# One table of a scan-and-MLP kernel: the clamp, the second block's first steps, two masks and the accumulator banks

## The chip, the cores and the metric

The kernel runs on one core of one Trainium2 chip. The core has a matrix engine (TensorE, PE in the profile, with its weight loads as PEld), three engines for elementwise work (VectorE or DVE, ScalarE or ACT, GpSimd or POOL), and a queue engine, SyncE or SP, that only issues DMAs. ScalarE and GpSimd can issue DMAs too. Each engine works through its own instruction stream in order and waits on semaphores for the others. The metric is the device time of one execution in microseconds (us).

## The reference

The inputs are a state-space scan followed by a squared-ReLU MLP. The scan is taken over chunks of 32 positions in the reference, with the state carried from chunk to chunk:

```python
log_a = np.log(np.clip(a, 1e-06, 1.0))
for c in range(nc):                                  # batch 4, 8 heads, 768 positions, head_dim 32, d_state 16
    cum = np.cumsum(la, axis=-1)
    L = np.exp(cum[:, :, :, None] - cum[:, :, None, :]) * causal
    y_intra = np.einsum('bhij,bhjd->bhid', np.einsum('bhin,bhjn->bhij', Cc, Bc) * L, xc)
    y_inter = np.einsum('bhin,bhnd->bhid', Cc, state) * np.exp(cum)[:, :, :, None]
    y[:, :, sl] = y_intra + y_inter
    state = decay_full[:, :, None, None] * state + np.sum(Bx, axis=2)
# y becomes 3072 tokens x 256; w_in is 256 x 2048, w_out 2048 x 256
h = np.maximum(x @ w_in, 0.0)
return (h * h @ w_out).astype(np.float32)
```

## The kernel before

**Tiling.** The work is cut into 12 units, each a batch and a stretch of 256 positions (`UNITS`). The first four units are the first stretch of the four batches. Each unit goes through a scan stage and then an MLP block; the blocks are lettered a to l, so block a is unit 0 and block b is unit 1.

**The order.** The string `ORDER` is the schedule, written out by hand. It is read token by token, and each token records its instructions on their engines. What stands earlier in the string stands earlier in the stream of each engine it uses, so the string sets the order on every engine and on every DMA queue. Nothing reorders it.

**The scan stage of a unit k**, by tokens:
- `ldC`, `ldB`, `ldx`: loads on SP's queue. `pc`, `pb`, `px`: GpSimd (or the engine named behind a colon: `v` VectorE, `a` ScalarE, `p` GpSimd) scales C by the running product of a, casts B, and divides x by that product, into the tiles jt and xs.
- `tr`, `tc`: PE transposes jt into a PSUM bank, and two engines copy it out to bct (L205, L220, L218).
- `mt`: the scores C·B, 16 matmuls (L235) into banks 0 to 3. Each bank has then to be multiplied by the causal mask. `mk` does it on VectorE straight from PSUM (L244). `sc` followed by `ms` does it in two steps: ScalarE copies the bank out (L249), and the engine named behind `ms` multiplies the copy (L253).
- `u`: 16 matmuls that give the unit's contribution to the state. `ina` and `inb`: 32 matmuls of masked scores with xs. `sf`: VectorE scales the state (tile Sd, L383). `ca`: two matmuls that add the carried state (all L260).
- `t`: two copies that take the result out of PSUM as the tile T, the input of the MLP block. `us`: the copy of the state.

**The MLP block**, by tokens: `b0` is step 0 of block b, four matmuls of 128x256 (L450) into one bank and the ReLU on ScalarE (L459, tile hb); `qb0` is the square on VectorE (L465, tile h); `B0` is the four matmuls with w_out (L481). A block has eight steps. Steps 0 and 1 use the first quarter of w_in (`w_in_b0`), steps 2 and 3 the second (`w_in_b1`), and so on.

**The weights** come in eight DMAs on GpSimd's queue, `wi0` to `wi3` (L148) and `wo0` to `wo3` (L152).

**The later rows of a.** Units 0 to 3 need only the first 64 rows of `a`. The other rows come in four small DMAs and are then prepared once: `ac1` clamps them (L604, GpSimd, tile a_cl), `sk1` takes the running product (L533, VectorE, tile cp), `pp1` picks the last column (L608, ScalarE), `p2` turns them on PE in fp32 (L507, L511, L620), and `pd` copies the result out (L626, L627, ScalarE).

**The banks.** `pp` is all of PSUM, eight banks of 512 fp32. `bank()` gives out the bank that has been free longest, in the order of the string. A digit behind `@` names the bank instead, and `u0:67` names the pair of banks of a `u`. `id` tokens are matmuls of ones, whose result nobody uses, that stand between the first steps.

Of the kernel before, what the change touches and what calls it, by code (L numbers as in the profile page):

```python
# [30 lines left out]
def kernel(  # L31
# [16 lines left out]
    ORDER = """  # L48
        fa1:a jz0:v ef jz1:p id3:512 ti fa0:s la0:s id4:512 pi eb ldB0:s ac0:v ldC0:a sk0 ku sp la1:a pbh0:p hd
        id1:256 pc0:v pbl0:v mb:a id2:512 trC0 ps iv:8:16 tcC0:1:a tcC0:0:v trB0 la2:s tcB0:2:v pk id1:512 iv1:0:8  # L50
        id1:512 ldx0:s mt0 wi0 la3:s px0:v ldC1:s ac1:p su id2:512 ldB1:s wi1 ldx1:s u0:67 mk0 fq mk0 mk0 pc1:p sc0
        pb1:a tr1 id2:512 tc1:1:a tc1:0:v jz2:a to ms0:p sf0 sk1 wo0 wi2 px1:p mt1 ina0 inb0 ca0 mk1 mk1 t0:aa sc1 us0
        pp1:a mk1 a0 ldC2:s a1 u1 ina1 ms1:v wo1 wi3 pc2 inb1 p2 pd sf1 ca1 t1:va us1 a3 qa1 ldB2:s qa0 a2 wo2 b0 qa3
        qb0 b1 qb1 fr b2 b3 A0 A1 B0 pb2:p B1 tr2 zb0 qb3 gB3:v ldx2:s ldB3:s ldC3:s ldx3:s b4 a4 iv:32:64 zb1 tc2:1:v
        qa2 tc2:0:v b5 sb1 sb0 qb4 a5 qb2 qa4 mt2 sc2 B3 iv:16:32 px2 mk2 mk2 sc2 A3 A2 ms2:v qa5 a6 b6 ms2:p B2 a7
        qb5 pb3:a qa6 b7 u2 ina2 inb2 sf2 wo3 pc3 px3 ld4 A4 tr3 ca2 tc3:1:v t2:aa B4 us2 B5 tc3:0:v u3:45 pc4 mt3 A5
        us3 sc3 c5 qb7 qb6 mk3 za3 pb4 ldC5:s ldB5:s c3 qa7 c4 qc5 c0 qc3 px4 tr4 ldx5:s pb5 pc5 sa3 c1 c6 ldC6:s tr5
        ldB6:s ldx6:s qc4 qc0 A6 px5 pq A7 wm c2 B6 c7 C0 ms3:v mk3 qc6 mk3 qc7 afC2 pc6 B7 C3 C6 C4 qc1 bk rg4 C1 qc2
        d1 d0 za4 sa4 pb6 mk4 mk4 d3 mk4 C5 d4 qd0 d2 mk4 px6 tr6 ld7 C2 C7 qd1 qd2 qd3 zb3 rg5 sb3 D0 mk5 za5 sa5 D1
        mk5 d5 qd4 D2 pc7 pb7 d6 qd5 d7 qd6 D3 zb2 e0 qd7 mk5 e1 qe0 sb2 D4 mk5 D5 tr7 ld8 e2 qe1 D6 e3 qe2 ml px7 rg6  # L60
        e4 D7 qe3 za6 sa6 zb6 mk6 e5 qe4 sb6 e6 qe5 e7 qe6 iv:64:96 mk6 E0 E1 E2 E3 ldC9:s ldB9:s px8 mk6 f0 qe7 E4 f1
        qf0 pc8 E5 pb8 tr8 ldx9:s E6 mk6 f2 qf1 f3 qf2 E7 rg7 mk7 F0 f4 qf3 za7 F1 F2 f5 qf4 f6 qf5 f7 qf6 g0 qf7 zb7
        sa7 sb7 mk7 F3 mk7 F4 pc9 pb9 tr9 px9 ld10 g1 qg0 F5 mk7 g2 qg1 zb4 sb4 F6 g3 qg2 F7 rg8 za8 zb8 sa8 sb8 g4
        qg3 G0 mk8 g5 qg4 G1 mk8 g6 qg5 G2 g7 qg6 G3 mk8 h0 qg7 G4 pc10 pb10 tr10 px10 ld11 h1 qh0 G5 mk8 zb5 sb5 h2
        qh1 G6 h3 qh2 G7 rg9 za9 zb9 sa9 sb9 h4 qh3 H0 mk9 h5 qh4 H1 mk9 h6 qh5 H2 h7 qh6 H3 mk9 i0 qh7 H4 pc11 pb11
        tr11 px11 i1 qi0 H5 mk9 i2 qi1 H6 i3 qi2 H7 rg10 za10 zb10 sa10 sb10 i4 qi3 I0 mk10 i5 qi4 I1 mk10 i6 qi5 I2
        i7 qi6 I3 mk10 j0 qi7 I4 j1 qj0 I5 mk10 j2 qj1 I6 j3 qj2 I7 rg11 za11 zb11 sa11 sb11 j4 qj3 J0 mk11 j5 qj4 J1
        mk11 j6 qj5 J2 j7 qj6 J3 mk11 k0 qj7 J4 k1 qk0 J5 mk11 k2 qk1 J6 k3 qk2 J7 rg12 k4 qk3 K0 k5 qk4 K1 k6 qk5 K2
        k7 qk6 K3 l0 qk7 K4 l1 ql0 K5 l2 ql1 K6 l3 ql2 K7 l4 ql3 L0 l5 ql4 L1 l6 ql5 L2 l7 ql6 L3 ql7"""
# [803 lines left out]
```

## Time and profile before

| | us |
|---|---|
| median of 3 runs | 114.66 |
| lowest and highest run | 114.01, 114.71 |
| the profiled execution's own time | 114.46 |
| its span in the profile | 112.8 |
| PE busy in the span | 107.3 |
| VectorE, ScalarE, GpSimd busy | 83.8, 77.0, 51.9 |

The span runs from the first instruction to the last. The profiled execution took 1.66 us more than its span and 0.20 us less than the median run. Busy time on PE is modelled from starts, so a busy PE isn't a PE at its peak. In a merged row of the timeline, several like instructions in a row stand as one, with their count behind an x.

### The profile page before, as it was taken

The page shows a single profiled execution, that of the slowest core. Times are in us where ns is not written, and L with a number is a line of the kernel's source. Part 1 is how long each engine was busy: PE and PEld are TensorE (multiplying, and loading weights), DVE is VectorE, ACT ScalarE, POOL GpSimd, SP SyncE. Part 2 cuts the span into 40 slices and gives each one's busy share as a digit, 9 for nine tenths or more (in the row PEclk, how much of TensorE's full clock was granted, in tenths as well). Part 3 has the DMA queues.
Part 4 walks back from the last instruction along what each step waited for, and adds up shares of the span by engine and source line. Part 5 has one row for each costly group of instructions (what it writes and reads, how often), then busy time and mean ns, then how long its engine had stood idle before and what let it go on. Part 6 is the DMA issues. An engine that isn't in the chain of part 4 may idle for free.

```text
span 112.8 us, 3680 instructions
## 1 busy us (share of the span) xinstructions
PE 107.3 (95%) x1450; PEld 92.3 (82%) x1450; DVE 83.8 (74%) x187; ACT 77.0 (68%) x158; POOL 51.9 (46%) x97
## 2 busy tenths in 40 slices
...
GB/s 39 196 192 180 188 216 202 130 195 182 149 164 58 117 255 97 112 173 74 109 167 76 179 140 83 143 147 110 184 123 0 6 96 0 21 78 0 93 0 93
DMA packets 67281, 13.44 MB, mean 119 GB/s; under 512 B 63104, under 2 KB 65984, under 8 KB 67264
## 3 DMA queue, kind: packets, MB, share of 16 engines
...
q10 hardware_dynamic: 1280, 0.23, 1.1%
q8 instruction: 11, 0.18, 0.8%
q14 instruction: 6, 0.05, 0.1%
...
## 4 chain that ended last, share of the span: by engine, by line
PE 74%; DMA 13%; SPq 6%; issue 3%; POOL 2%; ACT 0%; ACTq 0%; POOLq 0%
PE pp L481 34%; PE pp L450 32%; DMA x_nat<-in_x_dram 13%; PE pp L260 5%; SPq L134 4%; PE pp L229 2%; SPq L642 1%; PE pp L235 1%; POOL xs L187 1%; POOL jt L167 1%; SPq L117 0%; PE pp L205 0%; ACT osl L831 0%; POOL w_out_b L152 0%; POOL mts L253 0%
## 5 line engine op out<-in xcount | busy, mean ns | idle before, releaser
L459 ACT ACTIVATE hb<-pp 128x512 bf16<-128x512 f32 x96 | 54.8, 602 | 22.9 <-PE pp L450 22.6
L465 DVE TENSOR_TENSOR h<-hb 128x512 bf16<-128x512 bf16 x96 | 46.0, 494 | 13.9 <-ACT hb L459 13.3
L450 PE MATMUL pp<-T,w_in_b 128*128 128x256 bf16 x384 | 53.4, 273 | 1.2 <-ACT us L336 0.6
L481 PE MATMUL pp<-w_out_b,h 128*128 128x256 bf16 (+1 forms) x400 | 53.8, 268 | 0.0
L450 PEld LDWEIGHTS <-w_in_b 128*128 128x128 bf16 x384 | 41.4, 114 | 3.2 <-issue 1.3
L481 PEld LDWEIGHTS <-h 128*128 128x128 bf16 x400 | 37.6, 98 | 4.5 <-issue 1.0
L244 DVE TENSOR_TENSOR mts<-pp,mask 128x512 bf16<-128x512 f32 x43 | 28.6, 679 | 0.8 <-PE pp L229 0.8
L187 POOL TENSOR_TENSOR xs<-x_nat,Pinv 128x256 bf16<-128x256 f32 (+1 forms) x19 | 13.6, 727 | 11.4 <-PE pp L260 7.1
L371 POOL TENSOR_TENSOR Sd<-z,Pquad 128x256 bf16<-128x256 f32 x16 | 10.7, 678 | 15.0 <-DVE z L355 8.7
L167 POOL TENSOR_TENSOR jt<-C_nat,P_sb 128x128 bf16<-128x128 f32 x22 | 9.7, 463 | 6.0 <-DMA C_nat<-in_C_dram 6.0
L355 DVE SCALAR_TENSOR_TENSOR z<-z,Ptot,us 128x64 f32<-128x64 f32 x8 | 3.2, 406 | 5.6 <-ACT us L339 4.4
L540 PE MATMUL pp<-const-bfloat16-1.0 128*128 128x512 bf16 (+1 forms) x16 | 6.2, 520 | 0.8 <-PEq L857 0.8
L175 POOL CAST jt<-B_nat 128x256 bf16<-128x256 f32 x9 | 4.5, 505 | 5.0 <-DMA B_nat<-in_B_dram 5.0
L488 ACT COPY osb<-pp 128x512 f32<-128x512 f32 x11 | 6.4, 585 | 0.3 <-PE pp L481 0.2
L260 PE MATMUL pp<-mts,xs 64*32 64x128 bf16 (+1 forms) x288 | 5.5, 219 | 0.0
L260 PE MATMUL pp<-bct,Sd 128*128 128x128 bf16 x40 | 4.2, 220 | 0.0
L260 PEld LDWEIGHTS <-xs 64*32 64x32 bf16 (+1 forms) x288 | 3.6, 93 | 0.4 <-issue 0.2
L540 PEld LDWEIGHTS <-const-bfloat16-1.0 128*128 128x128 bf16 x16 | 1.6, 119 | 2.3 <-issue 2.2
L260 PEld LDWEIGHTS <-Sd 128*128 128x128 bf16 x40 | 3.0, 98 | 0.3
L148 POOL DMA_DIRECT2D w_in_b<-in_moe_w_in_dram x4 | 3.1, 782 | 0.3 <-issue 0.3
L249 ACT CAST sc<-pp 128x512 bf16<-128x512 f32 x5 | 2.9, 610 | 0.2 <-PE pp L235 0.2
L205 PEld LDWEIGHTS <-jt 128*128 128x128 bf16 x24 | 1.7, 104 | 1.6 <-POOL jt L167 0.8
...
## 6 DMA issues: line engine op xcount, KB each, us to landing
...
```

Source lines behind the costliest of these rows:

```text
L134: (eng or nc.sync).dma_start(out=t[what][:, hs[0]:hs[1]], in_=_dap(src, ((b * NH + hs[0]) * S + j * 256) * w, [[2 * w, 128], [S * w, hs[1] ...
L167: eng.tensor_tensor(out=_fap(jt[k % 3], 128 + 144 * g, [[384, 2], [32, 4], [1, 16]]), in0=_fap(loaded[k]["C"], 128 * g, [[16, 2], [32, 4], ...
L187: eng.tensor_tensor(out=_fap(xs, 256 * r, [[256, 2 // n], [32, 8], [1, 32]]), in0=_fap(loaded[k]["x"], 32 * r, [[32, 2 // n], [64, 8], [1, ...
L244: nc.vector.tensor_tensor(out=live[k]["mts"][:, q].rearrange("p r g i -> p (r g i)"), in0=pp[:, q, :], in1=mask1 if k >= LATE else mask, o ...
L260: nc.tensor.matmul(dst, w, v, start=bool(need), stop=False, skip_group_check=True, **({} if pos is None else {"tile_position": pos}))
L371: nc.gpsimd.tensor_tensor(out=_fap(S_d, 0, [[128, 2], [32, 4], [1, 32]]), in0=_fap(z, 0, [[32, 2], [0, 4], [1, 32]]), in1=_fap(Pquad, 4 * ...
L450: nc.tensor.matmul(pp[:, h, i * 256:(i + 1) * 256] if c is None else _fap(pp, h * 512 + i * 256 + c * 64, [[128, 2], [1, 64]]), _fap(w, g ...
L459: nc.scalar.activation(out=hb.rearrange("p i t -> p (i t)"), in_=pp[:, h, :], func=AF.Relu)
L465: nc.vector.tensor_tensor(out=h2, in0=hb, in1=hb, op=ALU.mult)
L481: nc.tensor.matmul(dst, h2[:, i, r * 128:(r + 1) * 128], w_out_b[gi][:, 2 * o + i, c0:c1], start=first, stop=(fp == 7 and i == 1), skip_gr ...
L488: nc.scalar.copy(out=osb, in_=pp[:, 6 if blk == 1 else 7, :])
L540: nc.tensor.matmul(pp[:, h, 0:int(cols)], ones_b[:, 0:128], ones_b[:, 0:int(cols)] if dep is None else dep, start=True, stop=True, skip_gr ...
```

## The change

Only the table `ORDER` is changed. It has 557 tokens before and after. The new table is a line longer, so every later line number goes up by one: L450 of before is L451 of the change.

```diff
-        id1:512 ldx0:s mt0 wi0 la3:s px0:v ldC1:s ac1:p su id2:512 ldB1:s wi1 ldx1:s u0:67 mk0 fq mk0 mk0 pc1:p sc0
-        pb1:a tr1 id2:512 tc1:1:a tc1:0:v jz2:a to ms0:p sf0 sk1 wo0 wi2 px1:p mt1 ina0 inb0 ca0 mk1 mk1 t0:aa sc1 us0
-        pp1:a mk1 a0 ldC2:s a1 u1 ina1 ms1:v wo1 wi3 pc2 inb1 p2 pd sf1 ca1 t1:va us1 a3 qa1 ldB2:s qa0 a2 wo2 b0 qa3
-        qb0 b1 qb1 fr b2 b3 A0 A1 B0 pb2:p B1 tr2 zb0 qb3 gB3:v ldx2:s ldB3:s ldC3:s ldx3:s b4 a4 iv:32:64 zb1 tc2:1:v
-        qa2 tc2:0:v b5 sb1 sb0 qb4 a5 qb2 qa4 mt2 sc2 B3 iv:16:32 px2 mk2 mk2 sc2 A3 A2 ms2:v qa5 a6 b6 ms2:p B2 a7
-        qb5 pb3:a qa6 b7 u2 ina2 inb2 sf2 wo3 pc3 px3 ld4 A4 tr3 ca2 tc3:1:v t2:aa B4 us2 B5 tc3:0:v u3:45 pc4 mt3 A5
+        id1:512 ldx0:s mt0 wi0 la3:s px0:v ldC1:s su id2:512 ldB1:s wi1 ldx1:s u0:67 mk0 fq mk0 mk0 pc1:p sc0 pb1:a
+        tr1 id2:512 tc1:1:a tc1:0:v jz2:a to ms0:p ac1:p sf0 wo0 px1:p wi2 mt1 ina0 inb0 ca0 mk1 mk1 t0:aa sc1 us0 mk1
+        a0 a1@1 ldC2:s u1:23 ina1 ms1:v wo1 inb1 sf1 ca1 t1:va sk1 us1 wi3 pc2 qa0 ldB2:s b0@0 qa1 pp1:a b1@2 wo2 qb0
+        a3@3 qb1 a2@1 p2@5 qa3 pd fr b2@4 b3@0 A0 A1 B0 pb2:p B1 tr2 zb0 qb3 gB3:v ldx2:s ldB3:s ldC3:s ldx3:s b4@1
+        a4@0 iv:32:64 zb1 tc2:1:v qa2 tc2:0:v b5@4 sb1 sb0 qb4 a5@5 qb2 qa4 mt2 sc2 B3 iv:16:32 px2 wo3 pc3 px3 mk2
+        mk2 sc2 A3 A2 ms2:v ms2:v qa5 a6@0 b6@1 pb3:a B2 a7@2 qb5 qa6 b7@3 u2 ina2 inb2 sf2 ld4 A4 tr3 ca2 tc3:1:v
+        t2:aa B4 us2 B5 tc3:0:v u3:45 pc4 mt3 A5
```

**First place: GpSimd, from the first weights' DMA on.** The rows name the line, the instruction, and the tiles with the unit's number (jt1 is unit 1's jt). Before:

```order
L148 DMA w_in_b0_113<-in_moe_w_in_dram 128x2x512
L604 TENSOR_SCALAR a_cl128_101<-a_nat128_99 128x128
L148 DMA w_in_b1_114<-in_moe_w_in_dram 128x2x512
L167 TENSOR_TENSOR jt1_111<-C_nat1_207,P_sb_106 128x2x4x16 x2
L253 TENSOR_TENSOR mts0_202<-sc0_3_240,mask_90 128x512
L152 DMA w_out_b0_117<-in_moe_w_out_dram 128x1024
L148 DMA w_in_b2_115<-in_moe_w_in_dram 128x2x512
L187 TENSOR_TENSOR xs1_262<-x_nat1_216,Pinv_107 128x512
```

The same place of the change:

```order
L149 DMA w_in_b0_113<-in_moe_w_in_dram 128x2x512
L149 DMA w_in_b1_114<-in_moe_w_in_dram 128x2x512
L168 TENSOR_TENSOR jt1_111<-C_nat1_207,P_sb_106 128x2x4x16 x2
L254 TENSOR_TENSOR mts0_202<-sc0_3_239,mask_90 128x512
L605 TENSOR_SCALAR a_cl128_101<-a_nat128_99 128x128
L153 DMA w_out_b0_117<-in_moe_w_out_dram 128x1024
L188 TENSOR_TENSOR xs1_260<-x_nat1_215,Pinv_107 128x512
L149 DMA w_in_b2_115<-in_moe_w_in_dram 128x2x512
```

The clamp has gone from ahead of the second weights' DMA to behind unit 0's mask, and unit 1's xs has gone ahead of the third weights' DMA.

**Second place: ScalarE, from unit 1's last score copy to the ReLU of step 3.** hb0_3 is the ReLU of block a, step 3, and hb1_0 that of block b, step 0. Before:

```order
L249 COPY sc1_2_320<-pp_121 128x512
L336 COPY us0_322<-pp_121 128x128
L608 ACTIVATE pick_p128_105<-pick_95,cp128_103 128x16
L459 ACTIVATE hb0_0_330<-pp_121 128x512
L459 ACTIVATE hb0_1_338<-pp_121 128x512
L626 COPY Ptot_108<-pp_121 128x16
L627 COPY P_sb_106<-pp_121 128x2x64
L218 COPY T1_407<-pp_121 128x4x64
L336 COPY us1_410<-pp_121 128x128
L459 ACTIVATE hb0_3_416<-pp_121 128x512
L459 ACTIVATE hb0_2_428<-pp_121 128x512
L459 ACTIVATE hb1_0_435<-pp_121 128x512
```

The same place of the change:

```order
L337 COPY us0_321<-pp_121 128x128
L460 ACTIVATE hb0_0_328<-pp_121 128x512
L460 ACTIVATE hb0_1_334<-pp_121 128x512
L219 COPY T1_392<-pp_121 128x4x64
L337 COPY us1_396<-pp_121 128x128
L460 ACTIVATE hb1_0_409<-pp_121 128x512
L609 ACTIVATE pick_p128_105<-pick_95,cp128_103 128x16
L460 ACTIVATE hb1_1_418<-pp_121 128x512
L460 ACTIVATE hb0_3_427<-pp_121 128x512
L460 ACTIVATE hb0_2_435<-pp_121 128x512
L627 COPY Ptot_108<-pp_121 128x16
L628 COPY P_sb_106<-pp_121 128x2x64
```

Steps 0 and 1 of block b now come ahead of steps 3 and 2 of block a, and the three instructions of the later rows have moved behind T1. PE has the same order: in the change the fp32 matmuls of `p2` (L508, L512, L621), which stood between `inb1` and `ca1`, stand between `a2` and `b2`. On VectorE the running product (`sk1`) has moved from ahead of unit 1's masks to behind T1's half.

**Third place: VectorE, unit 2's masks.** mts2 holds unit 2's masked scores, and h20_5 is the square of block a, step 5. Before:

```order
L244 TENSOR_TENSOR mts2_555<-pp_121,mask_90 128x512 x2
L253 TENSOR_TENSOR mts2_555<-sc2_0_556,mask_90 128x512
L465 TENSOR_TENSOR h20_5_578<-hb0_5_533 128x512
L465 TENSOR_TENSOR h21_5_603<-hb1_5_521 128x512
L465 TENSOR_TENSOR h20_6_606<-hb0_6_584 128x512
L383 TENSOR_TENSOR Sd2_0_662<-pp_121,Pquad_109 128x256
```

The same place of the change:

```order
L245 TENSOR_TENSOR mts2_555<-pp_121,mask_90 128x512 x2
L254 TENSOR_TENSOR mts2_555<-sc2_0_556,mask_90 128x512
L254 TENSOR_TENSOR mts2_555<-sc2_3_572,mask_90 128x512
L466 TENSOR_TENSOR h20_5_584<-hb0_5_533 128x512
L466 TENSOR_TENSOR h21_5_609<-hb1_5_521 128x512
L466 TENSOR_TENSOR h20_6_611<-hb0_6_590 128x512
L384 TENSOR_TENSOR Sd2_0_667<-pp_121,Pquad_109 128x256
```

VectorE has one mask more, which GpSimd did before. On GpSimd the last weights' DMA (`wo3`) and unit 3's jt and xs follow directly on unit 2's xs. The `@` digits change which bank a step writes, not where it stands.

More of the change, by code (lines that the diff above doesn't have):

```diff
@@ L55 @@
-        qa2 tc2:0:v b5 sb1 sb0 qb4 a5 qb2 qa4 mt2 sc2 B3 iv:16:32 px2 mk2 mk2 sc2 A3 A2 ms2:v qa5 a6 b6 ms2:p B2 a7
-        qb5 pb3:a qa6 b7 u2 ina2 inb2 sf2 wo3 pc3 px3 ld4 A4 tr3 ca2 tc3:1:v t2:aa B4 us2 B5 tc3:0:v u3:45 pc4 mt3 A5
-        us3 sc3 c5 qb7 qb6 mk3 za3 pb4 ldC5:s ldB5:s c3 qa7 c4 qc5 c0 qc3 px4 tr4 ldx5:s pb5 pc5 sa3 c1 c6 ldC6:s tr5
-        ldB6:s ldx6:s qc4 qc0 A6 px5 pq A7 wm c2 B6 c7 C0 ms3:v mk3 qc6 mk3 qc7 afC2 pc6 B7 C3 C6 C4 qc1 bk rg4 C1 qc2
-        d1 d0 za4 sa4 pb6 mk4 mk4 d3 mk4 C5 d4 qd0 d2 mk4 px6 tr6 ld7 C2 C7 qd1 qd2 qd3 zb3 rg5 sb3 D0 mk5 za5 sa5 D1
@@ L60 @@
[L60 to L69, printed above, removed]
+        id1:512 ldx0:s mt0 wi0 la3:s px0:v ldC1:s su id2:512 ldB1:s wi1 ldx1:s u0:67 mk0 fq mk0 mk0 pc1:p sc0 pb1:a
@@ new lines @@
+        t2:aa B4 us2 B5 tc3:0:v u3:45 pc4 mt3 A5 us3 sc3 c5 qb7 qb6 mk3 za3 pb4 ldC5:s ldB5:s c3 qa7 c4 qc5 c0 qc3 px4
+        tr4 ldx5:s pb5 pc5 sa3 c1 c6 ldC6:s tr5 ldB6:s ldx6:s qc4 qc0 A6 px5 pq A7 wm c2 B6 c7 C0 ms3:v mk3 qc6 mk3
+        qc7 afC2 pc6 B7 C3 C6 C4 qc1 bk rg4 C1 qc2 d1 d0 za4 sa4 pb6 mk4 mk4 d3 mk4 C5 d4 qd0 d2 mk4 px6 tr6 ld7 C2 C7
+        qd1 qd2 qd3 zb3 rg5 sb3 D0 mk5 za5 sa5 D1 mk5 d5 qd4 D2 pc7 pb7 d6 qd5 d7 qd6 D3 zb2 e0 qd7 mk5 e1 qe0 sb2 D4
+        mk5 D5 tr7 ld8 e2 qe1 D6 e3 qe2 ml px7 rg6 e4 D7 qe3 za6 sa6 zb6 mk6 e5 qe4 sb6 e6 qe5 e7 qe6 iv:64:96 mk6 E0
@@ new lines @@
+        E1 E2 E3 ldC9:s ldB9:s px8 mk6 f0 qe7 E4 f1 qf0 pc8 E5 pb8 tr8 ldx9:s E6 mk6 f2 qf1 f3 qf2 E7 rg7 mk7 F0 f4
+        qf3 za7 F1 F2 f5 qf4 f6 qf5 f7 qf6 g0 qf7 zb7 sa7 sb7 mk7 F3 mk7 F4 pc9 pb9 tr9 px9 ld10 g1 qg0 F5 mk7 g2 qg1
+        zb4 sb4 F6 g3 qg2 F7 rg8 za8 zb8 sa8 sb8 g4 qg3 G0 mk8 g5 qg4 G1 mk8 g6 qg5 G2 g7 qg6 G3 mk8 h0 qg7 G4 pc10
+        pb10 tr10 px10 ld11 h1 qh0 G5 mk8 zb5 sb5 h2 qh1 G6 h3 qh2 G7 rg9 za9 zb9 sa9 sb9 h4 qh3 H0 mk9 h5 qh4 H1 mk9
+        h6 qh5 H2 h7 qh6 H3 mk9 i0 qh7 H4 pc11 pb11 tr11 px11 i1 qi0 H5 mk9 i2 qi1 H6 i3 qi2 H7 rg10 za10 zb10 sa10
```

4 lines of the change are left out of this document (added).

## The prediction

> **What bounds the kernel now.** I read the page first, then PE's waits, then PE's timeline, then the timelines of the engines that PE waits for. The first lines of the page, and its chain:
>
> ```profile
> span 112.8 us, 3680 instructions
> PE 107.3 (95%) x1450; PEld 92.3 (82%) x1450; DVE 83.8 (74%) x187; ACT 77.0 (68%) x158; POOL 51.9 (46%) x97
> PE 74%; DMA 13%; SPq 6%; issue 3%; POOL 2%; ACT 0%; ACTq 0%; POOLq 0%
> ```
>
> PE is nearly always busy. The view of PE's waits, cut to the time from 14.4 us to the end, has a single row:
>
> ```profile
> PE pp L450 <- ACT us L336: 0.6, 1, 0.6
> ```
>
> That wait ends at 14.44 us. From there PE runs to its end without a wait that this view counts. So the time is made of three parts: when the dense stretch begins, how much PE work is left by then, and a tail. An edit is worth something only if it moves the begin or changes that work. PE's timeline (start, length, then line, tiles, shape and count) around the begin:
>
> ```profile
> 9.68 0.42 PE L235 MATMUL pp<-bct 32*64 32x256 bf16 x16
> 11.30 1.03 PE L450 MATMUL pp<-T,w_in_b 128*128 128x256 bf16 x8 [0.60 <-ACT T L218]
> 12.27 0.25 PE L260 MATMUL pp<-xs,jt 64*32 64x64 bf16 x16
> 12.34 0.65 PE L260 MATMUL pp<-mts,xs 64*32 64x128 bf16 x32
> 12.91 0.42 PE L507 MATMUL pp<-eye_f,cp 128*64 128x16 f32 x8
> 13.37 0.24 PE L620 MATMUL pp<-pick_p,spread 128*64 128x16 f32 x4
> 13.55 0.28 PE L260 MATMUL pp<-bct,Sd 128*128 128x128 bf16 x2
> 14.44 2.81 PE L450 MATMUL pp<-T,w_in_b 128*128 128x256 bf16 x24 [0.61 <-ACT us L336]
> 17.09 1.91 PE L481 MATMUL pp<-w_out_b,h 128*128 128x256 bf16 x16
> 18.84 0.50 PE L205 MATMUL pp<-eye_b,jt 128*128 128x128 bf16 x6
> 24.97 0.25 PE L260 MATMUL pp<-xs,jt 64*32 64x64 bf16 x16
> 26.02 0.73 PE L205 MATMUL pp<-eye_b,jt 128*128 128x128 bf16 x6
> 26.59 0.28 PE L260 MATMUL pp<-bct,Sd 128*128 128x128 bf16 x2
> ```
>
> The 24 matmuls from 14.44 to 17.09 take 0.110 each, so a step of four is 0.44. Two places matter. Before 14.44 PE stands still between `ca1` (13.55) and the first step of the dense stretch. And `tr3` at 26.02 takes 0.73 where `tr2` at 18.84 took 0.50, so 0.23 is lost inside the dense stretch. What released PE at 14.44 is seen from the weight loads and from ScalarE:
>
> ```profile
> 14.44 1.56 PEld L450 LDWEIGHTS <-w_in_b 128*128 128x128 bf16 x15 [0.78 <-DMA w_in_b<-in_moe_w_in_dram]
> 9.15 0.48 ACT L218 COPY bct<-pp 128x384 bf16<-128x384 bf16 x1 [1.22 <-PE pp L205]
> 10.60 0.65 ACT L218 CAST T<-pp 128x256 bf16<-128x256 f32 x2 [0.18 <-PE pp L260]
> 13.89 0.39 ACT L218 CAST T<-pp 128x256 bf16<-128x256 f32 x1
> ```
>
> The row of PE names ScalarE, but the weight load names the DMA: step a3 needs the second weights, which land just before 14.44. In the change, b0 stands first. It needs only the first weights, which step a0 used at 11.30, and T1, whose last half is ready at 13.89 + 0.39 = 14.28.
>
> **The begin of the dense stretch.** Block a's first step began 0.05 behind its T (10.60 + 0.65 = 11.25, then 11.30). With T1 as it is, b0 would begin at 14.33, a gain of 0.11. T1 hangs on `ca1`, that on `sf1`, that on `inb1`, and that on unit 1's masks. VectorE and GpSimd there:
>
> ```profile
> 9.14 0.35 DVE L220 COPY bct<-pp 128x384 bf16<-128x384 bf16 x1
> 9.74 0.42 DVE L533 TENSOR_TENSOR_SCAN cp<-a_cl,const-float32-0.0 128x128 f32<-128x128 f32 x1
> 10.14 1.89 DVE L244 TENSOR_TENSOR mts<-pp,mask 128x512 bf16<-128x512 f32 x3
> 11.95 0.58 DVE L253 TENSOR_TENSOR mts<-sc,mask 128x512 bf16<-128x512 bf16 x1
> 13.00 0.42 DVE L383 TENSOR_TENSOR Sd<-pp,Pquad 128x256 bf16<-128x256 f32 x1 [0.47 <-PE pp L260]
> 15.74 0.43 DVE L465 TENSOR_TENSOR h<-hb 128x512 bf16<-128x512 bf16 x1 [1.11 <-ACT hb L459]
> 6.37 0.65 POOL L604 TENSOR_SCALAR a_cl<-a_nat 128x128 f32<-128x128 f32 x1
> 7.89 0.77 POOL L167 TENSOR_TENSOR jt<-C_nat,P_sb 128x128 bf16<-128x128 f32 x2
> 11.03 1.07 POOL L187 TENSOR_TENSOR xs<-x_nat,Pinv 128x512 bf16<-128x512 f32 x1
> ```
>
> - The clamp takes 0.65 on GpSimd ahead of unit 1's jt. Without it jt ends near 8.0 instead of 8.66, and ScalarE's half of the bct copy (9.15 to 9.63, after 1.22 of waiting) can come as much earlier. VectorE's half can't: it stands behind unit 0's masks and ends at 9.49 either way. The scores started at 9.68, 0.05 behind ScalarE's half. They can now start near 9.58: **0.10 gained** of 0.65. The clamp itself then hides behind unit 0's mask, where GpSimd feeds nothing on PE's path.
> - The running product (0.42) leaves the front of unit 1's masks. It ended at 10.16, but the scores end at 9.68 + 0.42 = 10.10, so the masks could hardly have started before 10.14. I cost its removal at nothing by itself.
> - xs runs at 11.03 to 12.10 on GpSimd, into the last mask at 11.95, which took 0.58; a square of the same shape took 0.43. Now xs should be over before. Of these 0.15 PE sees 0.10 at most, because `ina1` of 12.34 stands ahead of the half that waits.
> - `p2` filled PE at 12.91 to 13.55, while it waited for Sd (13.00 + 0.42 = 13.42). `ca1` came 0.13 behind Sd, a little late because of `p2`; half of this, 0.05, comes back.
>
> With 0.11 + 0.10 + 0.05 + 0.05, where I take half of the mask's 0.10, the begin moves **0.3 earlier**, to 14.13. The bounds are 0.11, if nothing of the chain moves, and 0.99, if all passes through (0.11 + 0.65 + 0.10 + 0.13). ScalarE's b0, b1 and pick_p follow in an order in which each is ready: pick_p waits for the product, which now stands behind Sd and T1's half on VectorE (13.42 + twice 0.42 = 14.26), and `p2` comes after 16 matmuls, at 14.13 + 1.76 = 15.9. The named banks cost nothing: each was last read by a ReLU or copy a step or more ahead.
>
> **p2 in the dense stretch.** Its time in before was free, since PE waited for Sd anyway. From its first row at 12.91 to the next matmul at 13.55 it takes 0.64. A change from 128x128 tiles to small ones costs a step of its own: eight matmuls of 0.110 from 11.30 end at 12.18, and the next start at 12.27, so 0.09. Between a2 and b2 there is no wait to hide in, so `p2` costs **0.73**. The bounds: 0.46 (12.91 to 13.37, the issue alone) and 0.85.
>
> **The third masks.** At 23 to 26 us:
>
> ```profile
> 22.33 1.05 POOL L187 TENSOR_TENSOR xs<-x_nat,Pinv 128x512 bf16<-128x512 f32 x1 [1.68 <-DMA x_nat<-in_x_dram]
> 23.34 1.34 POOL L253 TENSOR_TENSOR mts<-sc,mask 128x512 bf16<-128x512 bf16 x1
> 25.25 1.04 POOL L167 TENSOR_TENSOR jt<-C_nat,P_sb 128x128 bf16<-128x128 f32 x2
> 22.92 0.74 DVE L253 TENSOR_TENSOR mts<-sc,mask 128x512 bf16<-128x512 bf16 x1
> 23.58 1.37 DVE L465 TENSOR_TENSOR h<-hb 128x512 bf16<-128x512 bf16 x1
> 25.96 0.41 DVE L383 TENSOR_TENSOR Sd<-pp,Pquad 128x256 bf16<-128x256 f32 x1
> ```
>
> GpSimd's mask of 1.34 goes, so unit 3's jt ends near 25.0 instead of 26.29, while PE reaches `tr3` at 26.45. The loss there goes: **0.23 back** (0 to 0.23). VectorE gains a mask of 0.58 to 0.74. But its square beside GpSimd's mask took 1.37 against 0.43 alone, and that falls to 0.43 or, beside the jt, a little over. The two nearly cancel, so Sd ends near 25.96 + 0.41 + 0.43 = 26.8, where `ca2` stands (26.59 + 0.2). I cost it at **nothing**, with 0.3 as the upper bound (each of the three squares 0.1 slower).
>
> The Trainium skill (GPSIMD Engine Reference, section 1, Specifications) says that GpSimd's SBUF interfaces are shared with VectorE, with contention for instructions in a 2-port mode or with two SBUF inputs. The 1.37 against 0.43 agrees, and the sum would be the same with it.
>
> **The DMAs.** The third weights' issue now has xs ahead of it. Their issue of before, and the time to landing:
>
> ```profile
> L148 POOL DMA_DIRECT2D w_in_b<-in_moe_w_in_dram x1: 706/706/706, 10.3 to 10.3; - x1
> DMA to landing us min/median/max: 7.7/7.7/7.7
> ```
>
> They landed at 18.0, and b4, which needs them, followed `tr2` at about 19.2. If xs's 1.07 passes through they land at 19.1, and b4 moves to 19.6: nothing, with 0.5 of cover. The second weights go out 0.65 earlier, the last ones about 1.3 earlier (the mask's time), and SP's order is as it was. Unit 2's load of x is the DMA that stands at 13% in the chain. It lands just before 22.33, its xs is ready at 23.38, and `u2` stands at 24.97, so it would have to slip by 1.6 before PE sees it. I cost these at nothing.
>
> **The sum.** −0.30 + 0.73 − 0.23 = **+0.20**. From the profiled execution's own 114.46 that is 114.66. This execution lies 0.20 under the median of 114.66, so the median to expect is **114.9**, a change within 1% (1.15 us, about what a measurement of this kernel can tell from no change). With every bound at its end the sum is between −0.99 + 0.46 − 0.23 = −0.76 and −0.11 + 0.85 + 0.3 = +1.04: 113.9 to 115.7.
>
> **The rivals.**
> - *p2 is absorbed.* If PE would wait in the new order at b2, because ScalarE's ReLUs are late, or if the small tiles overlap their neighbours, `p2` is free again. Then −0.30 − 0.23 gives 114.1, and with everything ahead in full (0.99) it is 113.4, over 1% faster. For it: ScalarE has the product's instructions in the middle of four ReLUs now. Against it: no bank or operand at b2 is late.
> - *VectorE becomes the bound, slower.* From 22.92 to 26.37 its rows stand without a gap, and it gets a mask more. If any work on GpSimd makes a square 1.37 long, and not the mask alone, the jt and xs that now follow do it too: Sd of unit 2 ends 0.44 + 0.66 later, at 27.5, and `ca2` waits to 27.6 instead of 26.8. That is +0.8, 115.7. With the two squares behind it also at 1.37 it is +2.5, 117.4. It decides when the three squares take more than about 1.7 together (the second mask ends at 22.92 + 0.44 + twice 0.66 = 24.7, and Sd must start by 26.4). Against it: beside GpSimd's jt two squares took 1.01 (24.95 to 25.96).
> - *The PE clock falls, slower.* With `p2` gone PE is idle around 13.0 to 13.4 as well as from 13.8 to 14.1, and the matmuls could go at half speed as at the start:
>
> ```profile
> 0.83 3.14 PE L540 MATMUL pp<-const-bfloat16-1.0 128*128 128x512 bf16 x7 [0.83 <-PEq L857]
> 5.95 0.60 PE L540 MATMUL pp<-const-bfloat16-1.0 128*128 128x512 bf16 x2
> ```
>
>   Seven took 0.45 each there, two took 0.30 each later, drain included. The slow part lasted from 0.83 to over 4 us; as much again at half speed would lose about 2 us: 116.9. Against it: gaps of 0.6 at 10.7 and 13.8 did nothing. The Trainium skill (TensorE: Matmul & The Clock Gate, part 1) asks for an idle window of about 3.4 us before the clock is halved; by that this rival can't happen, and the trace's gaps agree.
> - *The reorder does nothing,* since T1 is ready only 0.16 ahead of the second weights. That is the 0.11 bound of the sum, and lies in the forecast.
>
> **How the numbers follow.** Forecast 0.64, of it 0.01 over 1% slower. p2 absorbed 0.18, of it 0.07 over 1% faster. VectorE 0.12, of it 0.08 over 1% slower. Clock 0.04, slower. Something else 0.02, half slower. So faster 0.07, same 0.79, slower 0.14. The range takes in the forecast's bounds with a little of the spread of the runs (114.01 to 114.71), p2 absorbed without the full gain ahead, and VectorE's smaller price: 113.8 to 115.9.
>
> **What would show it.** Right: PE's first L451 of block b at 14.0 to 14.3, with a wait for ScalarE's T and none for a DMA; L508 to L621 near 15.9 with nothing idle around; six L206 of unit 3 in 0.50; VectorE's square at 24 us far under 1.37. Wrong: a PE wait inside the dense stretch, L451 steps over 0.44, or `p2` costing much less than 0.73 between a2 and b2.

## The result and the profile after

The changed kernel took 115.37 us (median of 20 runs, 114.23 to 117.54) and the kernel before 114.55 (20 runs, 113.37 to 116.02). The ratio is 1.0063, with a 95% interval of 1.0037 to 1.0089: 0.72 us slower, 0.42 to 1.02. The ratio leaves out runs in a slower state (6 of the change's 20), which is why it lies below the quotient of the two medians. The forecast was 114.9 us and +0.20.

The first lines of the page of the changed kernel, and its chain:

```profile
span 112.8 us, 3678 instructions
PE 106.8 (95%) x1450; PEld 92.1 (82%) x1450; DVE 81.9 (73%) x188; ACT 77.1 (68%) x158; POOL 50.2 (45%) x96
PE 92%; DVE 3%; ACT 1%; issue 1%; ACTq 0%
```

The span is that of before to a tenth, and the profiled execution's own time was 114.47 against 114.46. It is one of the fastest of its kernel, while the profiled execution of before stood near the median of its own. So the two traces, laid side by side, show less than the runs do, and this gap has to be explained as well. DMA, 13% of the chain of before, has gone from the chain.

PE's waits in the changed kernel, from 11.5 us to the end (line, releaser, total us, times, longest):

```profile
PE pp L261 <- DVE Sd L384: 0.5, 1, 0.5
PE pp L451 <- ACT T L219: 0.5, 1, 0.5
```

PE's timeline at the same places as in the prediction (start, length, line, tiles, shape, count, idle time before and its releaser):

```profile
9.48 0.42 PE L236 MATMUL pp<-bct 32*64 32x256 bf16 x16 [0.44 <-DVE bct L221]
11.11 1.03 PE L451 MATMUL pp<-T,w_in_b 128*128 128x256 bf16 x8 [0.59 <-ACT T L219]
...
13.22 0.28 PE L261 MATMUL pp<-bct,Sd 128*128 128x128 bf16 x2 [0.50 <-DVE Sd L384]
13.97 1.91 PE L451 MATMUL pp<-T,w_in_b 128*128 128x256 bf16 x16 [0.46 <-ACT T L219]
15.80 0.42 PE L508 MATMUL pp<-eye_f,cp 128*64 128x16 f32 x8
16.07 0.37 PE L512 MATMUL pp<-eye_f,cp 128*64 128x96 f32 x4
16.26 0.24 PE L621 MATMUL pp<-pick_p,spread 128*64 128x16 f32 x4
16.44 1.07 PE L451 MATMUL pp<-T,w_in_b 128*128 128x256 bf16 x8
17.34 1.91 PE L482 MATMUL pp<-w_out_b,h 128*128 128x256 bf16 x16
...
26.24 0.50 PE L206 MATMUL pp<-eye_b,jt 128*128 128x128 bf16 x6
26.57 0.28 PE L261 MATMUL pp<-bct,Sd 128*128 128x128 bf16 x2
```

The first step of block b starts at 13.97 and waits for ScalarE's T. `p2` stands at 15.80 to 16.44 with nothing idle around it. `tr3` takes 0.50. Against before, in the same order of places: the begin is 0.47 earlier (14.44 to 13.97), L482 at 17.34 is 0.25 later than L481 at 17.09, and behind `tr3` the two kernels are level again (26.57 and 26.59), as they stay to the end.

The second weights in the changed kernel are the second of these two DMAs; T1's last half on ScalarE and the third masks on VectorE follow:

```profile
L149 POOL DMA_DIRECT2D w_in_b<-in_moe_w_in_dram x2: 739/837/935, 5.2 to 6.1; - x2
DMA to landing us min/median/max: 5.4/5.8/6.2
```

```profile
13.54 0.37 ACT L219 CAST T<-pp 128x256 bf16<-128x256 f32 x1 [0.71 <-PE pp L261]
```

```profile
23.37 0.75 DVE L254 TENSOR_TENSOR mts<-sc,mask 128x512 bf16<-128x512 bf16 x2
24.04 1.50 DVE L466 TENSOR_TENSOR h<-hb 128x512 bf16<-128x512 bf16 x3
25.88 0.42 DVE L384 TENSOR_TENSOR Sd<-pp,Pquad 128x256 bf16<-128x256 f32 x1 [0.34 <-PE pp L261]
```

The weights land at 6.1 + 6.2 = 12.3, where before they landed at 14.4. That is 0.9 **ahead** of `ca1`. The step that stands first in the new order does not use them, and waits for T1 (13.54 + 0.37 = 13.91) instead. On VectorE the two masks take 0.75 together and the three squares 1.50, where before took 2.46 for the three.

### The profile page after: what moved, and what is told of

It reads as the page before. It is cut to its first block, busy times and chain, and to the rows that moved or that the text cites. A ratio compares the mean times of both kernels' runs of the same rounds, so it can differ in the third digit from the quotient of the medians.

```text
span 112.8 us, 3678 instructions
## 1 busy us (share of the span) xinstructions
PE 106.8 (95%) x1450; PEld 92.1 (82%) x1450; DVE 81.9 (73%) x188; ACT 77.1 (68%) x158; POOL 50.2 (45%) x96
## 4 chain that ended last, share of the span: by engine, by line
PE 92%; DVE 3%; ACT 1%; issue 1%; ACTq 0%
PE pp L451 38%; PE pp L482 38%; PE pp L261 7%; PE pp L541 4%; PE pp L230 2%; PE pp L236 2%; DVE mts L245 1%; ACT T L219 1%; PE pp L206 1%; DVE xs L188 1%; PE pp L518 1%; DVE bct L221 0%; DVE Sd L384 0%; PE pp L508 0%; ACT osl L832 0%
## 5 line engine op out<-in xcount | busy, mean ns | idle before, releaser
L451 PE MATMUL pp<-T,w_in_b 128*128 128x256 bf16 x384 | 53.5, 273 | 1.1 <-ACT T L219 1.1
L482 PE MATMUL pp<-w_out_b,h 128*128 128x256 bf16 (+1 forms) x400 | 53.8, 268 | 0.0
L466 DVE TENSOR_TENSOR h<-hb 128x512 bf16<-128x512 bf16 x96 | 43.4, 465 | 12.9 <-ACT hb L460 12.2
L451 PEld LDWEIGHTS <-w_in_b 128*128 128x128 bf16 x384 | 41.4, 114 | 3.0 <-issue 1.6
L482 PEld LDWEIGHTS <-h 128*128 128x128 bf16 x400 | 37.6, 98 | 4.5 <-issue 1.0
L188 POOL TENSOR_TENSOR xs<-x_nat,Pinv 128x256 bf16<-128x256 f32 (+1 forms) x19 | 13.9, 742 | 13.2 <-DMA x_nat<-in_x_dram 6.4
L372 POOL TENSOR_TENSOR Sd<-z,Pquad 128x256 bf16<-128x256 f32 x16 | 10.6, 667 | 13.9 <-DVE z L356 7.2
L221 DVE COPY bct<-pp 128x384 bf16<-128x384 bf16 (+1 forms) x7 | 2.2, 333 | 1.1 <-PE pp L206 0.6
```

The lines of the kernel that those rows point to most:

```text
L188: eng.tensor_tensor(out=_fap(xs, 256 * r, [[256, 2 // n], [32, 8], [1, 32]]), in0=_fap(loaded[k]["x"], 32 * r, [[32, 2 // n], [64, 8], [1, ...
L372: nc.gpsimd.tensor_tensor(out=_fap(S_d, 0, [[128, 2], [32, 4], [1, 32]]), in0=_fap(z, 0, [[32, 2], [0, 4], [1, 32]]), in1=_fap(Pquad, 4 * ...
L451: nc.tensor.matmul(pp[:, h, i * 256:(i + 1) * 256] if c is None else _fap(pp, h * 512 + i * 256 + c * 64, [[128, 2], [1, 64]]), _fap(w, g ...
L466: nc.vector.tensor_tensor(out=h2, in0=hb, in1=hb, op=ALU.mult)
L482: nc.tensor.matmul(dst, h2[:, i, r * 128:(r + 1) * 128], w_out_b[gi][:, 2 * o + i, c0:c1], start=first, stop=(fp == 7 and i == 1), skip_gr ...
```

## The experiments

All are edits of `ORDER`. The diffs show the words that move; words left out stay where they were. Ratios are to the kernel before, run on the same chip in the same hour, whose median was 114.69 beside the first four kernels, 114.56 beside the next four and 114.60 beside the last four.

### The change once more

No edit.

> The changed kernel once more, unchanged, for a second trace. Its first profiled execution took 114.47 us, 0.9 under its own median of 115.37, so that trace shows one of its best executions. Theory P (the fp32 matmuls p2 are the cost): +0.6 to +0.9 against the kernel before, and a slower execution begins block b's first step later than 13.97 us and has no wait behind it. Theory D (the DMAs are the cost): the same time, but a slower execution has a wait for a load inside the dense stretch, behind 14 us.

115.62 us, ratio 1.0085 (1.0047 to 1.0124). In its trace `ca1` starts at 13.78, b0 at 14.53 and `p2` takes 16.36 to 17.00; PE has the same two waits and no other. The loss is confirmed, a little over the 0.6 to 0.9 us expected. The begin of 13.97 is one of several.

### The third masks alone

```diff
-px2 mk2 mk2 sc2 A3 A2 ms2:v qa5 a6 b6 ms2:p B2 a7 qb5 pb3:a qa6 b7 u2 ina2 inb2 sf2 wo3 pc3 px3 ld4
+px2 wo3 pc3 px3 mk2 mk2 sc2 A3 A2 ms2:v ms2:v qa5 a6 b6 pb3:a B2 a7 qb5 qa6 b7 u2 ina2 inb2 sf2 ld4
```

> The kernel before with only the third-mask edits: unit 2's second copied mask on VectorE, and the last weights' DMA, unit 3's jt and xs ahead on GpSimd, unit 3's B cast ahead on ScalarE. P: -0.2 us, the 0.23 that tr3 lost, and nothing else. D, if the earlier DMA of the last weights is what hurts: +0.4 to +0.8.

114.97 us, ratio 1.0014 (0.9969 to 1.0058): no gain to be seen, though the 0.2 us expected lies inside the interval. PE's timeline:

```profile
13.52 0.29 PE L260 MATMUL pp<-bct,Sd 128*128 128x128 bf16 x2
13.92 2.81 PE L450 MATMUL pp<-T,w_in_b 128*128 128x256 bf16 x24
...
25.47 0.81 PE L205 MATMUL pp<-eye_b,jt 128*128 128x128 bf16 x6
```

`tr3` takes 0.81, more than the 0.73 of before, though GpSimd's mask has gone. In this execution the load of unit 2's x landed at 22.96, and GpSimd's xs could start only at 23.10. And the head of this kernel is that of before, instruction for instruction, yet a3 starts at 13.92: the second weights landed at 13.88 this time, not at 14.40.

### The swap of the steps alone

```diff
-us1 a3 qa1 ldB2:s qa0 a2 wo2 b0 qa3 qb0 b1 qb1 fr b2 b3
+us1 qa0 ldB2:s b0@0 qa1 b1@2 wo2 qb0 a3@3 qb1 a2@1 qa3 fr b2@4 b3@0
```

The steps up to a5 have the banks that the change names; `p2` and GpSimd's order are as before. Behind a5 this kernel has banks of its own: `bank()` gives a6, c5 and c3 the banks 3, 0 and 1, where before and the change both have 0, 4 and 5 (c is the third block).

> The kernel before with only steps 0 and 1 of block b put ahead of steps 3 and 2 of block a, with the banks named. The clamp, the product and p2 stay where they were, so p2 stands in its free place ahead of ca1. P: -0.1 us, from a begin at 14.33 instead of 14.44 in an execution like the one profiled, and more in executions where the second weights land late. D: -0.1 too, since GpSimd's DMAs are as before.

115.46 us, ratio 1.0080 (1.0040 to 1.0121): 0.92 us slower, where 0.1 faster was expected. PE, VectorE and GpSimd in its trace:

```profile
13.87 0.28 PE L261 MATMUL pp<-bct,Sd 128*128 128x128 bf16 x2
14.65 2.78 PE L451 MATMUL pp<-T,w_in_b 128*128 128x256 bf16 x24 [0.50 <-DVE h L466]
...
23.07 1.03 PE L451 MATMUL pp<-T,w_in_b 128*128 128x256 bf16 x8
...
29.07 0.60 PE L451 MATMUL pp<-T,w_in_b 128*128 128x256 bf16 x4
30.50 2.34 PE L451 MATMUL pp<-T,w_in_b 128*128 128x256 bf16 x20 [0.83 <-DVE mts L245]
```

```profile
27.52 2.33 DVE L466 TENSOR_TENSOR h<-hb 128x512 bf16<-128x512 bf16 x2
29.77 0.68 DVE L245 TENSOR_TENSOR mts<-pp,mask 128x512 bf16<-128x512 f32 x1
```

```profile
28.38 1.18 POOL L188 TENSOR_TENSOR xs<-x_nat,Pinv 128x256 bf16<-128x256 f32 x2
```

b0 starts 0.78 behind `ca1`, with the weights landed at 13.06. A step that needs no T1 follows `ca1` by 0.12 in other runs below, so the swap's own price here is 0.66. The rest of the loss is another thing, the banks. Scores stand in banks 0 to 3 until they are copied or masked. The steps a6 (23.07) and c5 (29.07) start 0.04 behind the end of ScalarE's copies of banks 3 and 0 (23.03 and 29.03), and lose 0.20 and 0.30 by it. The step c3 (30.50) starts 0.05 behind VectorE's mask of bank 1 (29.77 + 0.68 = 30.45), and that mask is late because the two squares at 27.52 took 2.33 beside GpSimd. Neither before nor the change has these steps in these banks, so the 0.92 us can't be read as the swap's price in the change.

### The change with the head of GpSimd as before

```diff
-ldC1:s su
+ldC1:s ac1:p su
-ms0:p ac1:p sf0 wo0 px1:p wi2
+ms0:p sf0 wo0 wi2 px1:p
```

> The changed kernel with GpSimd's first steps as before: the clamp ahead of the second weights' DMA, unit 1's xs behind the third weights' DMA. The product and p2 stay late, the masks stay as in the change. P: as slow as the change or slower, +0.6 to +1.1, because p2 stays in the dense stretch and the 0.1 to 0.2 that the earlier jt and xs brought are lost. D: the DMAs are as before up to 20 us, so at most +0.2.

116.30 us (6 runs), ratio 1.0178 (1.0113 to 1.0243): the slowest of all, 2.0 us over before where 0.6 to 1.1 was expected. Its b0 starts 0.75 behind `ca1`, at 14.09, so the begin does not explain the time. What its trace shows instead, on PE and on VectorE:

```profile
27.53 0.28 PE L261 MATMUL pp<-bct,Sd 128*128 128x128 bf16 x2 [0.68 <-DVE Sd L384]
```

```profile
24.37 2.77 DVE L466 TENSOR_TENSOR h<-hb 128x512 bf16<-128x512 bf16 x3
27.06 0.41 DVE L384 TENSOR_TENSOR Sd<-pp,Pquad 128x256 bf16<-128x256 f32 x1
```

This is the rival "VectorE becomes the bound" to the letter: three squares took 2.77 beside GpSimd's jt and xs, not beside a mask, and `ca2` waited to 27.53 (the rival said 27.6). It lost 0.84 by that. The profiled execution took 115.42 and is the fastest of the six, so what made the others slower still is not in the trace.

### p2 late, alone

```diff
-sf0 sk1 wo0 ... us0 pp1:a mk1 ... inb1 p2 pd sf1 ca1 t1:va us1 a3 qa1 ldB2:s qa0 a2 wo2 b0 qa3 qb0 b1 qb1 fr
+sf0 wo0 ... us0 mk1 ... inb1 sf1 ca1 t1:va sk1 us1 a3 qa1 ldB2:s qa0 pp1:a a2 wo2 b0 qa3 qb0 b1 qb1 p2 pd fr
```

> Before with p2 alone moved: the running product behind Sd on VectorE, pick_p behind it on ScalarE, p2's matmuls behind b1 in the dense stretch; block a's steps still first, GpSimd as before. Theory S (p2 costs its full 0.7 in the dense stretch, and the begin with a3 hangs on ca1 and the second weights, not on p2): 0.6 to 0.8 slower than before, ratio 1.005 to 1.007, the matmuls of L508 to L621 at 15 to 16 us with no wait around them. If p2 is absorbed there: within 0.2 of before. If VectorE's and GpSimd's collisions at 23 to 30 us carry the change's loss: within 0.2 of before as well, since nothing is moved there.

115.20 us, ratio 1.0061 (1.0019 to 1.0103): 0.70 us slower, where 0.6 to 0.8 was expected.

```profile
14.64 0.29 PE L260 MATMUL pp<-bct,Sd 128*128 128x128 bf16 x2 [0.54 <-DVE Sd L383]
14.77 1.91 PE L450 MATMUL pp<-T,w_in_b 128*128 128x256 bf16 x16
16.61 0.42 PE L507 MATMUL pp<-eye_f,cp 128*64 128x16 f32 x8
...
17.24 1.06 PE L450 MATMUL pp<-T,w_in_b 128*128 128x256 bf16 x8
```

Nothing waits around `p2`, so it is not absorbed. (The late start of this execution comes from matmuls at half speed at 11.48, where eight of L450 took 1.86: the granted clock was 0.50 from 10.5 to 13.9, and 1.0 around it.) With the weights landed at 13.23, a3 starts 0.13 behind `ca1`.

### The change with the old order of steps

```diff
-qa0 ldB2:s b0@0 qa1 pp1:a b1@2 wo2 qb0 a3@3 qb1 a2@1 p2@5 qa3 pd fr b2@4 b3@0
+a3@5 qa1 ldB2:s qa0 pp1:a a2@0 wo2 b0@1 qa3 qb0 b1@2 qb1 p2@3 pd fr b2@4 b3@5
```

> The change with block a's next steps a3 and a2 put back ahead of b0 and b1 (banks as before; GpSimd's order, late p2 and third masks as in the change). Theory S (b0 must wait for T1, 0.75 behind the start of ca1, while a3 needs only the second weights, which land earlier than 14.0 in most executions): a3 starts 0.4 behind ca1, and the kernel is 0.3 to 0.5 faster than the change, so 0.2 to 0.5 slower than before, ratio 1.002 to 1.004. If the swap does nothing or gains: as slow as the change or slower, ratio 1.006 to 1.009.

114.62 us, ratio 0.9999 (0.9961 to 1.0037). The change had 1.0063 and 1.0085 against its own runs of before, so undoing the swap alone takes back all of the loss, 0.7 to 1.0 us where 0.3 to 0.5 was expected.

```profile
13.00 0.28 PE L261 MATMUL pp<-bct,Sd 128*128 128x128 bf16 x2 [0.50 <-DVE Sd L384]
13.12 1.91 PE L451 MATMUL pp<-T,w_in_b 128*128 128x256 bf16 x16
...
26.16 0.28 PE L261 MATMUL pp<-bct,Sd 128*128 128x128 bf16 x2 [0.27 <-DVE Sd L384]
```

The banks of the steps that follow are those of before. a3 starts 0.12 behind `ca1`, not 0.4: with the weights landed at 12.40 nothing is left to wait for. Further on, at 26.16, `ca2` lost 0.44 to VectorE in this execution, where three squares took 2.35 together.

### The change with p2 back in its old place

```diff
-sf0 wo0 ... us0 mk1 ... wo1 inb1 sf1 ca1 t1:va sk1 us1 wi3 pc2 qa0 ldB2:s b0@0 qa1 pp1:a b1@2 ... a2@1 p2@5 qa3 pd fr
+sf0 sk1 wo0 ... us0 pp1:a mk1 ... wo1 wi3 pc2 inb1 p2 pd sf1 ca1 t1:va us1 qa0 ldB2:s b0@0 qa1 b1@2 ... a2@1 qa3 fr
```

> The change with the running product, pick_p and p2 back in their old places ahead of Sd and ca1; swap, GpSimd's order and third masks as in the change. Theory S: 0.6 to 0.8 faster than the change, so within 0.2 of before, ratio 0.999 to 1.002, with b0 still waiting for T1. If p2 is absorbed in the change: as slow as the change, ratio 1.006 to 1.009.

114.83 us, ratio 1.0023 (0.9982 to 1.0064), as expected within the interval.

```profile
13.82 0.28 PE L261 MATMUL pp<-bct,Sd 128*128 128x128 bf16 x2
14.60 2.78 PE L451 MATMUL pp<-T,w_in_b 128*128 128x256 bf16 x24 [0.50 <-ACT T L219]
```

Again b0 stands 0.78 behind `ca1`, while the weights had landed at 12.43.

### GpSimd's order and the masks, without swap and late p2

Both edits of the two kernels above at once, with the banks of before. It ran twice.

> What is left of the change when both the old order of steps and the old place of p2 are back: GpSimd's clamp behind its mask, xs ahead of the third weights, third masks on VectorE. Theory S: the second weights go out 0.65 earlier, a3 follows ca1 within 0.45, the dense stretch begins at 13.8 or earlier; 0.2 to 0.5 faster than before, ratio 0.996 to 0.998, and 1.0 to 1.2 faster than the change. If swap and p2 are not the cause (VectorE and GpSimd collide on the moved masks): still 0.4 or more slower than before, with a PE wait for VectorE's Sd or masks at 26 to 31 us.

> The version without swap and late p2 again, since its profiled execution was one with x landing late (PE waited 2.4 for GpSimd's xs). Theory W: ratio 0.990 to 0.996 again; in a profile with x landed by 11.4, the dense stretch begins with a3 0.13 behind ca1 near 13.5 and the span is 111.5 to 112.0. If the gain of the first time was chance: 0.997 or more.

First 114.11 us, ratio 0.9922 (0.9874 to 0.9970); then 114.29 us, ratio 0.9969 (0.9932 to 1.0006). The two intervals overlap from 0.993 to 0.997. In both traces a3 starts 0.12 behind `ca1`, as expected, but `ca1` itself is late (14.22 and 14.81), so the begin near 13.5 was a miss, and the second ratio lies above the 0.990 to 0.996 expected. The reason for the late `ca1`, on GpSimd in the second trace:

```profile
12.51 1.04 POOL L188 TENSOR_TENSOR xs<-x_nat,Pinv 128x512 bf16<-128x512 f32 x1 [1.76 <-DMA x_nat<-in_x_dram]
```

Unit 1's x landed at 12.37, where it had landed at 10.29 in the trace of before, and everything behind GpSimd's xs came late, the issue of the third weights too.

### The clamp alone

```diff
-ldC1:s ac1:p su
+ldC1:s su
-ms0:p sf0
+ms0:p ac1:p sf0
```

> Before with the clamp of the later a rows alone moved behind GpSimd's mask. Theory W (the clamp held up the issue of the second weights and unit 1's jt by 0.65 each, and with a3 first the begin hangs on whichever of the weights and ca1 is last): second weights issued near 6.1 to 6.3 and landed by 13.1, a3 starts 0.13 to 0.2 behind ca1, 0.5 to 0.9 faster than before, ratio 0.992 to 0.996. If the clamp is worth only the 0.10 of the prediction's chain and the gain lies in the masks and xs: within 0.2 of before, ratio 0.998 to 1.001.

114.31 us, ratio 0.9966 (0.9933 to 0.9998): 0.39 us faster (0.02 to 0.77).

```profile
12.86 0.25 PE L260 MATMUL pp<-xs,jt 64*32 64x64 bf16 x16 [0.82 <-POOL xs L187]
...
14.10 0.28 PE L260 MATMUL pp<-bct,Sd 128*128 128x128 bf16 x2
14.22 2.78 PE L450 MATMUL pp<-T,w_in_b 128*128 128x256 bf16 x24
```

The weights were issued at 6.18 and landed at 12.98, and a3 follows `ca1` by 0.12. Here too x landed late (11.62), and PE waited 0.82 for GpSimd's xs. The gain is under the 0.5 to 0.9 expected, and over the 0.10 of the prediction, but its interval reaches into both.

### The clamp and xs

As the clamp alone, and unit 1's xs ahead of the third weights:

```diff
-wo0 wi2 px1:p
+wo0 px1:p wi2
```

> Before with both GpSimd edits of the head: clamp behind the mask, unit 1's xs ahead of the third weights' issue; masks, swap and p2 as before. Theory W: as the clamp alone, or 0.1 to 0.2 better since xs is out of the way of unit 1's last mask: ratio 0.990 to 0.995, third weights landed near 17.5 to 18.5 without a PE wait for them. If the third masks are part of the gain of 0.45 that the version without swap and late p2 showed: ratio 0.996 to 1.000.

113.66 us (6 runs), ratio 0.9911 (0.9877 to 0.9944): 1.02 us faster than before, as expected. It beats both kernels.

```profile
13.67 0.29 PE L260 MATMUL pp<-bct,Sd 128*128 128x128 bf16 x2
13.79 2.78 PE L450 MATMUL pp<-T,w_in_b 128*128 128x256 bf16 x24
...
25.31 0.50 PE L205 MATMUL pp<-eye_b,jt 128*128 128x128 bf16 x6
```

`tr3` takes 0.50 although the third mask is still on GpSimd: unit 2's x landed at 16.90 and xs started at 21.30, a microsecond ahead of before.

### Before, looked at once more

No edit.

> The kernel before, unchanged, profiled once more. If its profiled execution of 14.44 was one with the second weights landing late: weights land between 13.0 and 14.1 this time and a3 starts at 13.6 to 14.1. If they always end the begin: a3 at 14.3 to 14.6, again directly behind the weights' landing.

```profile
13.60 0.28 PE L260 MATMUL pp<-bct,Sd 128*128 128x128 bf16 x2
14.16 2.81 PE L450 MATMUL pp<-T,w_in_b 128*128 128x256 bf16 x24 [0.28 <-DMA w_in_b<-in_moe_w_in_dram]
```

The weights landed at 14.12 and a3 started at 14.16. The truth lies between the two expectations: a3 stands directly behind the landing again, but the landing moves. This execution took 115.92 in all, which few runs of before reach. Behind the begin it has waits that the first trace of before has not, 0.47 for GpSimd's mask at 25.63 and 0.65 for VectorE's mask at 31.41 among them.

## Why the prediction came out as it did

The sign, the class (within 1%) and the range were right; the size was not (+0.20 against +0.72). The sum had three terms. The traces let them be measured apart, since PE has few waits behind the begin. "Rest" is the time from the first step of the dense stretch to the end of PE's last matmul. The two executions of GpSimd's order with masks aren't in the table, for x landed late in them:

| kernel | p2 | first step | ca1 | weights landed | begin | behind ca1 | rest |
|---|---|---|---|---|---|---|---|
| before | early | a3 | 13.55 | 14.40 | 14.44 | 0.90 | 95.39 |
| before, second look | early | a3 | 13.60 | 14.12 | 14.16 | 0.56 | 97.12 |
| third masks alone | early | a3 | 13.52 | 13.88 | 13.92 | 0.41 | 95.44 |
| clamp alone | early | a3 | 14.10 | 12.98 | 14.22 | 0.12 | 95.10 |
| clamp and xs | early | a3 | 13.67 | 13.70 | 13.79 | 0.12 | 95.09 |
| p2 late alone | late | a3 | 14.64 | 13.23 | 14.77 | 0.12 | 95.98 |
| old order of steps | late | a3 | 13.00 | 12.40 | 13.12 | 0.12 | 96.30 |
| swap alone | early | b0 | 13.87 | 13.06 | 14.65 | 0.79 | 96.59 |
| change, p2 early | early | b0 | 13.82 | 12.43 | 14.60 | 0.78 | 95.10 |
| change, old GpSimd head | late | b0 | 13.34 | 13.63 | 14.09 | 0.75 | 96.70 |
| change | late | b0 | 13.22 | 12.28 | 13.97 | 0.75 | 95.85 |
| change, again | late | b0 | 13.78 | 13.10 | 14.53 | 0.75 | 95.85 |

The shortest rest is 95.10, to 0.01 the same in three kernels. The other rows are, to 0.06, this, 0.75 more with `p2` late, and what PE loses in the trace: at `tr3` 0.23 in before, 0.31 with the third masks alone and 0.13 with `p2` late alone; at `ca2` 0.44 with the old order of steps and 0.84 with the old GpSimd head; and by its banks 0.20, 0.30 and 0.99 with the swap alone. The second look, with the waits named above, wasn't taken apart.

**The begin, −0.30: this is the step that failed.** Its mechanism was right: in all five traces that have b0 first it starts 0.75 to 0.79 behind `ca1`, and 0.05 behind the end of T1's last half, with no DMA named. So T1 holds it, and not its bank. At 13.97 it even came 0.16 before the forecast. What it was measured against was wrong. With a3 first the begin is 0.04 behind the weights' landing or 0.12 behind `ca1`, whichever is later, and before's 14.44 is the latest of three executions with the same head (14.44, 14.16, 13.92, mean 14.17). The change's two begins, 13.97 and 14.53, have a mean of 14.25. So the begin moved by about +0.1, as far as two and three executions that differ by 0.5 can tell. The prediction noted that the second weights "go out 0.65 earlier" and cost that at nothing; in fact it takes away the wait that the swap was to fill. With the weights there in time a3 can follow `ca1` by 0.12, and b0 only by 0.75: the swap gives 0.63 away. With it undone the change fell from 1.0063 and 1.0085 to 0.9999. By itself it cost 0.92 us (0.46 to 1.39), but there its own banks add to it. The change's banks cost nothing behind the begin: its rest with `p2` early is 95.10, as with the clamp alone, which names none of them. "T1 is ready only 0.16 ahead of the second weights", which the prediction put into a bound, was the weakest line of the sum: it is a difference of two times of which one moves by 0.5 between executions.

**p2, +0.73: right.** The change's rest is 95.10 with `p2` early and 95.85 with it late, so 0.75, and neither has a wait behind the begin. The kernel with `p2` late alone lost 0.70 (0.22 to 1.18). The rival that it is absorbed is out.

**The third masks, −0.23: right in the trace, for a reason that is half of what decides.** `tr3` took 0.50 in the change. But the masks alone brought nothing to be seen (+0.16, −0.36 to +0.66) with `tr3` at 0.81, and `tr3` took 0.50 in three traces with the mask still on GpSimd. With the mask gone unit 3's jt does end earlier, as forecast: 2.6 to 2.9 behind the start of unit 2's xs in six of eight traces, against 3.9 to 4.0 in the six with the mask in place. Whether PE sees this depends on when that xs can start, and so, among other things, on when unit 2's x lands. In the fourteen traces it landed at 22.0 to 23.0 four times, all with the clamp in its old place, and by 18.9 the other ten times, two of them with the clamp in its old place. Why, was not tried.

**GpSimd's clamp and xs, 0.15 of the 0.30: far too small** where a3 stands first. They brought 1.02 us (0.64 to 1.41). Of this the trace shows 0.30 in the rest and, at the begin, 0.65 against before's own trace but 0.38 against the mean of three. By the mean 0.34 stays open. Waits like those of the second look at before, which the first trace lacks, may be part of it; no run shows it. With b0 first they were worth about as much (1.0178 against 1.0063 and 1.0085), and there the begin shows none of it; the one trace shows 0.85 in the rest (96.70 against 95.85) instead.

**The sum again.** GpSimd's order and the masks, without swap and late `p2`, had 0.9922 and 0.9969. The traces' 0.63 for the swap and 0.75 for `p2` make 1.38 us, or 1.2%, and lead from there to 1.004 and 1.009; the change had 1.0063 and 1.0085. From the traces of before and the change, the begin's +0.1 and the rest's 95.85 − 95.4 = +0.45 make +0.55; what is missing to 0.72 lies within the interval. That the forecast lay near is luck, for two errors met: the swap, taken as a gain of 0.11, is a loss, and GpSimd's edits, taken as 0.15, gain far more.

**The other rivals.** VectorE as the bound came true in the traces of two variants: at the place and price foretold with the old GpSimd head (0.84), and with 0.44 in the old order of steps. It did in neither of the change's two traces. The prediction asked whether any work on GpSimd slows a square, or the mask alone. Any does: see below.

The clock stayed full in the change's two traces (1.0 and 0.996 over the span). But the prediction held this rival impossible without an idle window of about 3.4 us, and the trace of `p2` late alone differs from that: the granted clock was 0.50 from 10.5 to 13.9, and PE's longest wait in the 3.4 us before was 0.91. Here the measurement decides. Four of the change's 32 runs had a mean granted clock of 0.985 and took 117.5 to 118.2. Of the 87 runs of before beside the experiments 13 had 0.985 or less and took 114.6 to 116.4. So a fall is no more frequent in the change; why it cost more there, no trace shows.
